# The output's store, the sums for 1/z and the split of the scaled output: three moves in the order of a pooled-attention and SoLU-FFN kernel

## The chip, the core and the metric

The kernel runs on one core of one Trainium2 chip. The metric is the device time of one execution in microseconds (us); lower is better. The engines are named as the profile names them: PE is the matrix engine (TensorE) and PEld its weight loads, DVE is VectorE, ACT is ScalarE, POOL is GpSimd, and SP is the engine whose queue issues nearly all DMAs here; SPq marks its issuing instructions.

## What is computed

```python
kv_flat = kv.reshape(B, H//4, 4, W//4, 4, C).mean(axis=(2, 4)).reshape(B, -1, C) @ w_sr
s = q @ kv_flat.T / sqrt(C)
a = exp(s - s.max(-1)); a /= a.sum(-1) + 1e-9
x = a @ kv_flat
h = x @ w_in
e = exp(h - h.max(-1))
solu = h * e / (e.sum(-1) + 1e-9)
ln = (solu - mean(solu)) / sqrt(var(solu) + 1e-6) * g_ln
out = ln @ w_out
```

There are 4 batches of 12288 queries of 128 features; pooling leaves 768 keys per batch; the hidden width is 1024. All is float32 outside the kernel. Inside, most products are made of a high and a low 16-bit part, so that one product in float32 becomes three in 16 bits.

## The kernel before

The 49152 queries are cut into 384 tiles of 128, and four tiles make a group; there are 96 groups, 24 to a batch. One loop runs over 384 slots. A slot holds the work of one tile in every stage, and each stage is some slots behind the one ahead of it, so that a slot works on some ten different tiles. What follows says which stage works on which tile in the slot `slot`, with `t` for the tile.

- **Scores.** PE multiplies queries by keys into PSUM (`scores_pe`, L386, tile slot + 1). DVE takes the row's maximum `nm` (L402), ACT takes the exponential and its sum `z` (L403) and writes the high half of `phl` (L407), DVE writes the low half (`scores_split`, L415). SP turns `phl` into `pT` by a DMA transpose (`scores_turn`, L422). The four transposes of a group go out in the slots that are 1, 2 and 3 modulo 4, two of them in the last.
- **Values.** PE multiplies `pT` by the values for a whole group at once, in four quarters over four slots (`values`, tile `xa`, L453). The first quarter stands in the slot that is 1 modulo 4 and needs the group's last `pT`, which was issued two slots before. ACT and DVE split the result into `xh` (L459) and `xl` (L464).
- **1/z.** For a group, POOL forms `zz` from `z` (`values_norm`, L479), DVE takes the reciprocal `rz` (`values_recip`, L487), and ACT derives a third column of it (`values_recip_u`, L492). The constant `NORM = 6` puts all three six slots after the slot of the group's last tile, in one that is 1 modulo 4: one slot ahead of the first use of `rz`.
- **Hidden.** PE makes `h` (`hidden_pe`, L505, tile slot - 9). DVE takes the least of the scaled row (`hidden_max`, tile `junkd`, L513, tile slot - 10), ACT the exponential `e` (L529), DVE the product `u` (`hidden_u`, L543, tile slot - 11), ACT the variance (`junk`, L603), and POOL splits `u` into two halves of `uhl` (L560, L566). SP turns `uhl` into `uT` by a DMA transpose (`hidden_turn`, L580).
- **Output.** PE multiplies `uT` by `w_out` into one PSUM bank per group (`final_pe`, tile `o`, L631, tile slot - 13). DVE scales the bank into `ob` in two instructions (`final_half`, L674): tiles 0 and 1 of the group in the slot that is 0 modulo 4, ahead of the product of tile 3, and tiles 2 and 3 in the next slot. Behind the second, SP stores the group's 256 KB (`final_store`, L685).

In the last slot of every group SP also loads the queries of a later group (`q_load`, L345). For batches 1 to 3, keys come in 16 loads of 384 KB each (`kv_load`, L216), begun while the batch before is still worked on; POOL adds them up, and PE, ACT and POOL make keys and values of them in slots listed in `PLAN`.

There is no scheduler: each engine's instructions run in the order in which the loop's body calls the helpers, and SP's DMAs are issued in that order, one queue, first in first out. A DMA whose data isn't ready holds up all those behind it. After slot 383 a hand-written list, `TAIL`, gives the order of what is left.

PSUM: `s` and `h` share three buffers of two banks each, in turn. So PE's `s` of a slot waits for DVE's `u` of the same slot, and PE's `h` of a slot waits for DVE's low half of `phl` of that slot. `xa` and `o` have one bank each. Of `ob` there are two buffers.

Of the kernel before, what the change touches and what calls it, by code (L numbers as in the profile page):

```python
# [21 lines left out]
P = 128  # L22
# [23 lines left out]
XSP = 5  # L46
NORM = 6
LH = 10
LO = 13
# [7 lines left out]
TAIL = """  # L57
U:-1 xa:-1 xh:-1 h:1 o:-4 M:0 xl:-1 J:-1 h:2 hi:-1 E:0 lo:-1 M:1 zz:-1 E:1 o:-3 U:0 h:3
J:0 U:1 zz:0 hi:0 rc:-1 h:4 M:2 ob:-3 rc:0 hi:1 f2:-2 lo:0 rz:-1 E:2 turn:-1 xa:0 turn:0
# [18 lines left out]
def kernel(  # L78
# [63 lines left out]
    state = {}  # L142
# [526 lines left out]
    def final_half(g, half):  # L669
        _, f = state["f", g]  # L670
        if half == 0:
            state["ob", g, 0] = dmt.tile([P, GT, P], F32, tag="ob", name=f"ob_{g}_0")
        js = slice(half * 2, half * 2 + 2)
        nc.vector.scalar_tensor_tensor(  # L674
            state["ob", g, 0][:, js],
            state["po", g][:, half * 256 : half * 256 + 256].rearrange("p (j c) -> p j c", j=2),
            swi,
            f[:, js].unsqueeze(2).to_broadcast([P, 2, P]),
            op0=ALU.mult,
            op1=ALU.mult,  # L680
        )

    def final_store(g, j0=0, j1=GT):
        t0, n = g * GT + j0, j1 - j0
        nc.sync.dma_start(  # L685
            out[t0 * P : (t0 + n) * P, :].rearrange("(j p) c -> p j c", p=P),
            state.pop(("ob", g, j0)),
        )

    def final_out(g):  # L690
        final_half(g, 1)
        final_store(g)

# [182 lines left out]
    def at_last(t, fn, *args):  # L876

        if 0 <= t < NT and t % GT == GT - 1:
            fn(t // GT, *args)

    def at_soon(t, fn):

        at_last(t, fn) if t >= GT else fn(0) if t == GT - 2 else None
# [8 lines left out]
    for slot in range(NT):  # L892
# [20 lines left out]
        at(slot + 1, scores_pe)  # L913
        at_soon(slot - NORM, values_norm)
        at_last(slot - FSC, final_scale)
# [22 lines left out]
        if slot >= LH:  # L938
# [3 lines left out]
            elif slot > LH:  # L942
                for t in (slot - 1, slot):
                    if t > LH and (t % GT == GT - 1) == (t == slot):
                        scores_turn(t)
        at_soon(slot - NORM, values_recip)
        at_soon(slot - NORM, values_recip_u)
        at(i + 1, hidden_pe)
# [5 lines left out]
        at(i - 1, hidden_turn)  # L954
        at_last(slot - LO - 1, final_out)
        at_last(slot - XSP, values_out)
        for st in todo:
# [3 lines left out]
            elif len(st) == 1 and st[0].func not in (*FRONT, *BETWEEN, kv_load):  # L961
                st[0]()
        if slot % GT == GT - 1:
            q_load(slot // GT + 3)
        for st in todo:
# [65 lines left out]
```

## Time and profile before

| | us |
|---|---|
| median of 3 runs | 1854.53 (1848.84 to 1858.07) |
| the profiled execution | 1848.9 |
| its span | 1847.1 |

| engine | busy us | share of the span |
|---|---|---|
| PE | 1821.1 | 99% |
| DVE | 1784.9 | 97% |
| ACT | 1752.8 | 95% |
| POOL | 1613.8 | 87% |

A matmul counts as busy until its modelled end, and the next one starts before that, so PE's share is an upper bound of its work. The granted clock of PE is at full speed in all 40 slices of the span. Issuing a DMA doesn't count as busy: how full SP's queue is has to be read from the timeline of its issues. A row of the timeline gives the start, the duration, the engine, the line, the operation, the tiles written and read, and how many instructions were merged; in brackets the idle time ahead of it and what ended that. A row of the waits gives the total, the number of waits and the longest.

### The profile page before, as it was taken

The numbers are of one execution on the slowest core, as the hardware profiler recorded it, in microseconds if no ns is written. First come the engines' busy times: TensorE is split into PE (matmuls) and PEld (weight loads), VectorE is DVE, ScalarE is ACT, GpSimd is POOL, SyncE is SP. The second block draws the span as 40 slices with busy tenths as digits, with TensorE's granted clock in tenths as the row PEclk, the third lists the DMA queues.
The fourth block names the chain that finished last, engine by engine and source line by source line (L and its number), as shares of the span: only waits on it lengthen the run. The fifth ranks groups of instructions, "written<-read, shape, count | busy, mean of one in ns | idle before, by whom it ended". The sixth has DMA issues, their size and how long they took to land.

```text
span 1847.1 us, 43152 instructions
## 1 busy us (share of the span) xinstructions
PE 1821.1 (99%) x15717; PEld 1179.2 (64%) x15718; DVE 1784.9 (97%) x2729; ACT 1752.8 (95%) x3148; POOL 1613.8 (87%) x1392
## 2 busy tenths in 40 slices
PE   8999999999999999999999999999999999999999
PEld 4566666666666666666666666666666666666666
DVE  7999999999999999999999999999999999999998
ACT  6999999999999999999999999999999999999998
POOL 3899889899998999989988899989888888888887
PEclk9999999999999999999999999999999999999999
DMA  8999999999999999999999999999999999999998
GB/s 300 208 238 233 229 245 234 236 240 245 232 234 240 244 238 241 235 233 238 235 233 234 247 241 241 238 236 231 227 217 230 233 228 223 230 227 231 224 223 179
DMA packets 1473253, 431.80 MB, mean 234 GB/s; under 512 B 1400977, under 2 KB 1454353, under 8 KB 1472785
## 3 DMA queue, kind: packets, MB, share of 16 engines
q1 hardware_dynamic: 1472752, 428.98, 114.1%
q8 instruction: 124, 2.03, 0.5%
q14 instruction: 89, 0.72, 0.1%
q10 hardware_dynamic: 288, 0.07, 0.0%
HBM read 52.50 MB, written 25.17 MB: 42 GB/s over the span
## 4 chain that ended last, share of the span: by engine, by line
PE 63%; DVE 13%; ACT 7%; POOL 7%; issue 7%; DMA 3%; DVEq 0%; POOLq 0%; ACTq 0%
PE o L631 19%; PE h L505 18%; PE xa L453 13%; PE s L386 13%; DVE junkd L513 3%; DVE nm L402 3%; POOL uhl L566 3%; DVE phl L415 2%; ACT e L529 2%; DMA pT<-phl 2%; ACT junk L603 2%; POOL uhl L560 2%; ACT phl L407 2%; DVE u L543 1%; DVE ob L674 1%
## 5 line engine op out<-in xcount | busy, mean ns | idle before, releaser
L566 POOL TENSOR_TENSOR uhl<-u,uhl 128x1024 f16<-128x1024 f32 x382 | 815.1, 2134 | 31.7 <-ACT uhl L558 0.2
L631 PEld LDWEIGHTS <-uT 128*128 128x128 f16 x9072 | 537.1, 98 | 91.9 <-DMA uT<-uhl 7.0
L631 PE MATMUL o<-wch,uT 128*128 128x128 f16 x6048 | 568.0, 219 | 1.3 <-DMA uT<-uhl 1.3
L631 PE MATMUL o<-wcl,uT 128*128 128x128 f16 x3024 | 525.9, 219 | 0.0
L560 POOL TENSOR_SCALAR uhl<-u 128x1024 f16<-128x1024 f32 x377 | 393.5, 1044 | 136.2 <-DVE u L543 131.1
L543 DVE SCALAR_TENSOR_TENSOR u<-h,rz,e 128x1024 f32<-128x1024 f32 x384 | 491.2, 1279 | 16.0 <-ACT e L529 3.6
L513 DVE TENSOR_SCALAR_CACHE_REDUCE junkd<-h,rz 128x1024 bf16<-128x1024 f32 x384 | 491.5, 1280 | 1.4 <-PE h L505 1.0
L529 ACT ACTIVATE e<-h,nm,rz 128x1024 f32<-128x1024 f32 x384 | 459.0, 1195 | 1.0 <-DVE junkd L513 1.0
L603 ACT ACTIVATE junk<-u,su 128x1024 bf16<-128x1024 f32 x384 | 437.8, 1140 | 0.2 <-DVE u L543 0.2
L402 DVE TENSOR_REDUCE nm<-s 128x1 f32<-128x768 f32 x384 | 365.7, 952 | 23.3 <-PE s L386 20.8
L453 PE MATMUL xa<-pT,vh 128*128 128x512 f16 x1152 | 373.5, 379 | 6.6 <-DMA pT<-phl 4.0
L403 ACT ACTIVATE s<-s,nm 128x768 f32<-128x768 f32 x384 | 335.9, 875 | 41.9 <-DVE nm L402 37.1
L415 DVE SCALAR_TENSOR_TENSOR phl<-s,phl 128x768 f16<-128x768 f32 x384 | 366.3, 954 | 4.5 <-ACT phl L407 4.3
L407 ACT ACTIVATE phl<-s 128x768 f16<-128x768 f32 x384 | 311.0, 810 | 11.7
L505 PEld LDWEIGHTS <-xh 128*128 128x128 f16 x1536 | 144.8, 97 | 191.7 <-issue 26.7
L386 PE MATMUL s<-kh,qh 128*128 128x384 f32 x768 | 248.0, 404 | 0.1
L505 PE MATMUL h<-w_in_h,xh 128*128 128x512 f16 x768 | 228.2, 379 | 3.5 <-DVE rz L487 2.4
L505 PE MATMUL h<-w_in_h,xl 128*128 128x512 f16 x768 | 228.4, 379 | 0.0
L505 PE MATMUL h<-w_in_l,xh 128*128 128x512 f16 x768 | 228.3, 379 | 0.0
L453 PE MATMUL xa<-pT,vl 128*128 128x512 f16 x576 | 218.3, 379 | 0.0
L386 PE MATMUL s<-kc,ql 128*128 128x384 bf16 x768 | 187.8, 326 | 7.4 <-DVE phl L415 4.4
L386 PE MATMUL s<-kl,qf 128*128 128x384 bf16 x768 | 192.2, 332 | 0.1
(127 smaller groups left out, 1707.2 us busy)
## 6 DMA issues: line engine op xcount, KB each, us to landing
kv<-in_kv_dram SPq DMA_DIRECT2D x64, 384.0 KB, 4.3
qf<-in_q_dram SPq DMA_DIRECT2D x96, 256.0 KB, 3.3
out_dram<-ob SPq DMA_DIRECT2D x95, 256.0 KB, 2.8
pT<-phl SPq DMA_TRANSPOSE x384, 3.8
uT<-uhl SPq DMA_TRANSPOSE x378, 4.4
raw_in<-in_moe_w_in_dram SPq DMA_DIRECT2D x1, 1024.0 KB, 5.4
raw_out<-in_moe_w_out_dram SPq DMA_DIRECT2D x1, 1024.0 KB, 8.6
out_dram<-ob SPq DMA_DIRECT2D x1, 192.0 KB, 2.0
```

The costliest lines, as they stand in the source:

```text
L386: nc.tensor.matmul(s[:, half, :384], lh[:, ts], rh[:, half * 384 : (half + 1) * 384], start=n == (t == 0), stop=n == 2,)
L402: nc.vector.tensor_reduce(nm, s, axis=AX.XY, op=ALU.max, negate=True)
L415: nc.vector.scalar_tensor_tensor(phl[:, 1], state.pop(("s", t)), SC, phl[:, 0], op0=ALU.mult, op1=ALU.subtract)
L453: nc.tensor.matmul(xa, v[:, c, :], pT[:, :, a * NKC + c, :], start=n == 0, stop=n == len(seq) - 1)
L505: nc.tensor.matmul(h[:, hs], lh[:, ts], rh[:, hs], start=n == 0, stop=n == 2)
L513: nc.vector.tensor_scalar(junk, state["h", t], state["rz", g][1][:, j : j + 1], None, op0=ALU.mult, op1=ALU.min, accum_out=nm,)
L529: nc.scalar.activation(e, state["h", t], AF.Exp, bias=nm, scale=state["rz", g][0][:, js], accum_out=state["z2", g][:, js],)
L543: nc.vector.scalar_tensor_tensor(u, state.pop(("h", t)), state["rz", g][2][:, j : j + 1], state.pop(("e", t)), op0=ALU.mult, op1=ALU.mult, ...
L560: nc.gpsimd.tensor_scalar(uhl[:, 0, :], u, 1.0, 1.0, op0=ALU.mult, op1=ALU.mult)
L566: nc.gpsimd.tensor_tensor(uhl[:, 1, :], u, uhl[:, 0, :], op=ALU.subtract)
L603: nc.scalar.activation(junk, u, AF.Square, scale=-float(DFF), bias=su, accum_out=state["v3", g][:, j : j + 1],)
L631: nc.tensor.matmul(po[:, ts], uT[:, a * NFC + c, :], w[:, c, :], start=start, stop=stop)
```

## The change

Three things move, and no instruction is added or taken away:

- The store of a group goes out two slots later, in the slot that is 3 modulo 4, behind that slot's transposes and ahead of the load of queries.
- `zz` is formed three slots sooner, in the slots 2 modulo 4, and `rz` (DVE) and its third column (ACT) one slot sooner, in the slots 0 modulo 4. In DVE's order the reciprocal now stands ahead of the first piece of the scaled output instead of ahead of the second.
- The output is scaled in pieces of three tiles and one instead of two and two.

```diff
-NORM = 6
+ZSUM = 3
+ZREC = 5
...
-        js = slice(half * 2, half * 2 + 2)
+        j0, n = ((0, 3), (3, 1))[half]
+        js = slice(j0, j0 + n)
         nc.vector.scalar_tensor_tensor(
             state["ob", g, 0][:, js],
-            state["po", g][:, half * 256 : half * 256 + 256].rearrange("p (j c) -> p j c", j=2),
+            state["po", g][:, j0 * P : (j0 + n) * P].rearrange("p (j c) -> p j c", j=n),
             swi,
-            f[:, js].unsqueeze(2).to_broadcast([P, 2, P]),
+            f[:, js].unsqueeze(2).to_broadcast([P, n, P]),
...
-    def final_out(g):
-        final_half(g, 1)
-        final_store(g)
...
-        at_soon(slot - NORM, values_norm)
+        at_soon(slot - ZSUM, values_norm)
...
-        at_soon(slot - NORM, values_recip)
-        at_soon(slot - NORM, values_recip_u)
+        at_soon(slot - ZREC, values_recip)
+        at_soon(slot - ZREC, values_recip_u)
...
-        at_last(slot - LO - 1, final_out)
+        at_last(slot - LO - 1, final_half, 1)
...
         if slot % GT == GT - 1:
+            at_last(slot - LO - 3, final_store)
             q_load(slot // GT + 3)
```

In `TAIL` the step `zz:-1` is gone, because the loop now reaches it. All rows of the orders below are of the first batch; a number behind a tile's name is its tile or group, and the one behind that can be passed over.

SP's queue before, from one load of queries to the next (the store is that of group 13, the `pT` that of group 17):

```order
L345 DMA qf_19_4726<-in_q_dram 128x512
L580 DMA_TRANSPOSE uT_57_4793<-uhl_57_4745 128x16x128
L216 DMA kv_2_1_4798<-in_kv_dram 128x768
L422 DMA_TRANSPOSE pT_17_4758<-phl_68_4732 128x12x128
L580 DMA_TRANSPOSE uT_58_4875<-uhl_58_4820 128x16x128
L685 DMA out_0_dram<-ob_13_0_4767 128x4x128
L422 DMA_TRANSPOSE pT_17_4758<-phl_69_4803 128x12x128
L580 DMA_TRANSPOSE uT_59_4946<-uhl_59_4898 128x16x128
L422 DMA_TRANSPOSE pT_17_4758<-phl_70_4885 128x12x128
L422 DMA_TRANSPOSE pT_17_4758<-phl_71_4951 128x12x128
L580 DMA_TRANSPOSE uT_60_5017<-uhl_60_4967 128x16x128
L345 DMA qf_20_5019<-in_q_dram 128x512
```

The same stretch of SP's queue in the change:

```order
L346 DMA qf_19_4730<-in_q_dram 128x512
L581 DMA_TRANSPOSE uT_57_4801<-uhl_57_4749 128x16x128
L217 DMA kv_2_1_4806<-in_kv_dram 128x768
L423 DMA_TRANSPOSE pT_17_4762<-phl_68_4736 128x12x128
L581 DMA_TRANSPOSE uT_58_4875<-uhl_58_4824 128x16x128
L423 DMA_TRANSPOSE pT_17_4762<-phl_69_4811 128x12x128
L581 DMA_TRANSPOSE uT_59_4949<-uhl_59_4901 128x16x128
L423 DMA_TRANSPOSE pT_17_4762<-phl_70_4884 128x12x128
L423 DMA_TRANSPOSE pT_17_4762<-phl_71_4954 128x12x128
L581 DMA_TRANSPOSE uT_60_5020<-uhl_60_4970 128x16x128
L687 DMA out_0_dram<-ob_13_0_4775 128x4x128
L346 DMA qf_20_5023<-in_q_dram 128x512
```

The store has passed five transposes: three of `pT`, among them the group's last (`phl_71`), and two of `uT` (59 and 60). What stands behind the load of queries has the same work ahead of it as before.

DVE before, in the slots 100 and 101, from the first piece of the scaled output to the second and the maximum behind it:

```order
L674 SCALAR_TENSOR_TENSOR ob_21_0_7135<-o_21_6924,swi_100,f2_21_7040 128x256
L402 TENSOR_REDUCE nm_101_7168<-s_101_7106 128x1
L543 SCALAR_TENSOR_TENSOR u_90_7173,su_90_7174<-h_90_7061,rz_22_6893,e_90_7121 128x1024
L464 SCALAR_TENSOR_TENSOR xl_23_7165<-xa_23_6906,xh_23_7163 128x512
L513 TENSOR_SCALAR junkd_91_7194,nm2_91_7193<-h_91_7128,rz_22_6893 128x1024
L415 SCALAR_TENSOR_TENSOR phl_101_7171<-s_101_7106,phl_101_7171 128x768
L487 RECIPROCAL rz_23_7185<-zz_23_7184 128x8
L674 SCALAR_TENSOR_TENSOR ob_21_0_7135<-o_21_6924,swi_100,f2_21_7040 128x256
L402 TENSOR_REDUCE nm_102_7248<-s_102_7177 128x1
```

The same stretch of DVE in the change:

```order
L488 RECIPROCAL rz_23_6973<-zz_23_6972 128x8
L676 SCALAR_TENSOR_TENSOR ob_21_0_7143<-o_21_6924,swi_100,f2_21_7043 128x384
L403 TENSOR_REDUCE nm_101_7176<-s_101_7110 128x1
L544 SCALAR_TENSOR_TENSOR u_90_7181,su_90_7182<-h_90_7064,rz_22_6680,e_90_7125 128x1024
L465 SCALAR_TENSOR_TENSOR xl_23_7173<-xa_23_6910,xh_23_7171 128x512
L514 TENSOR_SCALAR junkd_91_7198,nm2_91_7197<-h_91_7136,rz_22_6680 128x1024
L416 SCALAR_TENSOR_TENSOR phl_101_7179<-s_101_7110,phl_101_7179 128x768
L676 SCALAR_TENSOR_TENSOR ob_21_0_7143<-o_21_6924,swi_100,f2_21_7043 128x128
L403 TENSOR_REDUCE nm_102_7247<-s_102_7185 128x1
```

The reciprocal and 128 elements of the scaled output have gone from between `phl_101` and `nm_102` to the place ahead of `nm_101`.

## Rows read from the trace of the kernel before

**Rows 1.** Page, part 1: busy time, share of the span and instructions of each engine.
```profile
PE 1821.1 (99%) x15717; PEld 1179.2 (64%) x15718; DVE 1784.9 (97%) x2729; ACT 1752.8 (95%) x3148; POOL 1613.8 (87%) x1392
```

**Rows 2.** Windows: busy us by engine, granted clock, DMA share, GB/s; key loads until 1240.
```profile
117.00:1240.00 1123.00, 1113.09 (x9687) 721.63 (x9686) 1094.93 (x1675) 1074.39 (x1929) 1020.05 (x879) 1.00 1.19 238
1240.00:1786.00 546.00, 545.41 (x4776) 355.92 (x4774) 536.73 (x823) 528.35 (x949) 465.26 (x394) 1.00 1.13 227
```

**Rows 3.** Waits of PE from 117 to 1240 us: total us, times, longest us.
```profile
PE xa L453 <- DMA pT<-phl: 4.0, 8, 1.0
PE xa L453 <- DVE ob L674: 2.2, 2, 1.1
PE o L631 <- DMA uT<-uhl: 1.3, 4, 0.5
PE h L505 <- DVE rz L487: 1.1, 4, 0.4
```

**Rows 4.** Waits of PE from 1240 to 1786 us, the only row.
```profile
PE h L505 <- DVE rz L487: 0.6, 2, 0.4
```

**Rows 5.** Timeline of SP's issues from a store on, and the store four groups later.
```profile
946.63 0.53 SPq L685 DMA_DIRECT2D out_dram<-ob  x1
947.26 1.47 SPq L422 DMA_TRANSPOSE pT<-phl  x1
...
956.81 0.53 SPq L345 DMA_DIRECT2D qf<-in_q_dram  x1
957.45 2.68 SPq L580 DMA_TRANSPOSE uT<-uhl  x1
...
1021.92 0.53 SPq L685 DMA_DIRECT2D out_dram<-ob  x1
```

**Rows 6.** Page, part 6: DMA issues, KB each, median us to landing.
```profile
kv<-in_kv_dram SPq DMA_DIRECT2D x64, 384.0 KB, 4.3
out_dram<-ob SPq DMA_DIRECT2D x95, 256.0 KB, 2.8
```

**Rows 7.** Timeline of DVE in one group without loads of keys, and the next group's first.
```profile
1453.98 0.96 DVE L402 TENSOR_REDUCE nm<-s 128x1 f32<-128x768 f32 x1
1455.07 1.28 DVE L543 SCALAR_TENSOR_TENSOR u<-h,rz,e 128x1024 f32<-128x1024 f32 x1
...
1458.35 0.47 DVE L674 SCALAR_TENSOR_TENSOR ob<-o,swi,f 128x256 f32<-128x256 f32 x1
1458.74 0.94 DVE L402 TENSOR_REDUCE nm<-s 128x1 f32<-128x768 f32 x1
...
1462.61 0.95 DVE L415 SCALAR_TENSOR_TENSOR phl<-s,phl 128x768 f16<-128x768 f32 x1
1463.48 0.19 DVE L487 RECIPROCAL rz<-zz 128x8 f32<-128x8 f32 x1
1463.59 0.43 DVE L674 SCALAR_TENSOR_TENSOR ob<-o,swi,f 128x256 f32<-128x256 f32 x1
1463.94 0.95 DVE L402 TENSOR_REDUCE nm<-s 128x1 f32<-128x768 f32 x1
...
1472.50 0.96 DVE L402 TENSOR_REDUCE nm<-s 128x1 f32<-128x768 f32 x1
```

**Rows 8.** Timeline of PE in the same group: scores, values and hidden products.
```profile
1458.16 0.50 PE L386 MATMUL s<-kl,qf 128*128 128x384 bf16 x2
...
1463.45 0.38 PE L453 MATMUL xa<-pT,vh 128*128 128x512 f16 x1
1463.71 0.59 PE L505 MATMUL h<-w_in_h,xh 128*128 128x512 f16 x2
```

**Rows 9.** Timeline of ACT in the same group: the end of an exponential, and `xh`.
```profile
1454.77 0.19 ACT L529 ACTIVATION_READ_ACCUMULATOR e<-h,nm,rz 128x1 f32 x1
...
1459.35 0.60 ACT L459 ACTIVATE xh<-xa 128x512 f16<-128x512 f32 x1 [0.17 <-PE xa L453]
```

**Rows 10.** Timeline of POOL in the same group: the split of `u`.
```profile
1466.18 1.04 POOL L560 TENSOR_SCALAR uhl<-u 128x1024 f16<-128x1024 f32 x1 [1.94 <-DVE u L543]
```

More of the change, by code (lines that the diff above doesn't have):

```diff
@@ L57 @@
 TAIL = """
-U:-1 xa:-1 xh:-1 h:1 o:-4 M:0 xl:-1 J:-1 h:2 hi:-1 E:0 lo:-1 M:1 zz:-1 E:1 o:-3 U:0 h:3
+U:-1 xa:-1 xh:-1 h:1 o:-4 M:0 xl:-1 J:-1 h:2 hi:-1 E:0 lo:-1 M:1 E:1 o:-3 U:0 h:3
 J:0 U:1 zz:0 hi:0 rc:-1 h:4 M:2 ob:-3 rc:0 hi:1 f2:-2 lo:0 rz:-1 E:2 turn:-1 xa:0 turn:0
```

## The prediction

> **What bounds the kernel now.** The page's busy times come first: PE has 99% of the span, DVE 97%, ACT 95% [rows 1]. No engine has room, so the time can only come out of PE's waits, and the next view is PE's waits by stretch. I cut the span where the loads of keys end, near 1240 us. Ahead of it PE waits 4.0 + 2.2 + 1.3 + 1.1 = 8.6 us in 18 waits [rows 3]; behind it, to 1786 us, 0.6 us in 2 [rows 4]. These rows understate: a matmul is drawn for 0.38 us while the next starts 0.21 later (two together last 0.59 [rows 8]), so a wait shows up to 0.17 us short. With 18 × 0.17 = 3.1 the first stretch holds at most 11.7 us of waits. Of the 18, 10 are of `xa`, and the largest row names its cause: the transposed scores `pT` had not landed. The second `xa` row names DVE's `ob`, which `xa` doesn't read; I count it as the same lateness.
>
> Why `pT` is late is read from two more views. The timeline of SP's issues shows stores at 946.63 and, four groups later, at 1021.92 [rows 5]: 18.82 us per group. Between them the issues stand end to end, with about 0.1 us between one and the next (947.26 follows 946.63 + 0.53); there is no gap in which the queue waits for data. The timeline of DVE in a group without loads of keys gives the pace that the engines can hold: from 1453.98 to 1472.50, 18.52 us [rows 7]. So from 117 to 1240 us the DMA queue is the slowest, by 0.30 us per group, and PE's waits are this difference showing whenever PE has used up its lead. A sum of bytes agrees. A group issues four transposes of 384 KB and four of 512 KB (128 × 12 × 128 and 128 × 16 × 128 halves of 2 bytes), a store and a load of queries of 256 KB each, and two loads of keys of 384 KB [rows 6] in every three groups: 4352 KB, or 4.46 MB. At the 238 GB/s that moved there [rows 2] that is 18.7 us. Without keys it is 4.19 MB, at 227 GB/s 18.5 us: the queue then merely keeps up with PE.
>
> **The change part by part.** *The store.* It keeps its 256 KB and its issue; five transposes pass it. In a queue that is never empty they go out sooner by what the store holds it up, at least its issue (947.26 - 946.63 = 0.63 us [rows 5]), at most its share by bytes (262 KB at 238 GB/s = 1.1 us). I take 1.1, since the queue is short of transfer and not of issues. But the queue's total per group is the same, and what stands behind the load of queries (two `uT`, the keys, the first `pT`) is as late as before. A queue of 18.82 us per group still lets PE do one group in 18.82. What is gained is lead: the `xa` that PE catches up with last may come 1.1 us sooner, once, and that lead stays to the end, because behind 1240 us PE hardly waits. So -1.1 us, not -1.1 per group. The lower end is 0, if one of the two `uT` that gain nothing is what PE catches up with last (4 of its waits are on `uT` already); the upper end is all 11.7 us, if the order and not the bytes made the queue slow. SP is also moved past one wait: `ob` is long done when the store now comes up, so the store can't hold the queue. `ob` is held two slots longer; its buffer is wanted again only two groups on, and the store lands in 2.8 us [rows 6].
>
> *The reciprocal and the third tile on DVE.* The reciprocal takes 0.11 us of DVE's order (1463.48 to 1463.59), a piece of two tiles 0.35 (1463.59 to 1463.94), and `phl` with 768 elements 0.87 (1462.61 to 1463.48) [rows 7]: 0.52 more for 512 more elements, about 0.13 for a tile. So 0.11 + 0.13 = 0.24 us go from behind `phl` in the slots 1 modulo 4 to ahead of `nm` in the same slots. DVE's sum is unchanged. Now `nm` starts at 1458.74, 0.39 behind the first piece; in the change at 1458.35 + 0.11 + 0.35 + 0.13 = 1458.94, 0.20 later. From there to the end of `phl` at 1463.56 DVE has no gap, and PE's `h` at 1463.71 waits for that end: the `xa` ahead of it began at 1463.45 and would have let `h` start at 1463.66 [rows 8]. So in the first such group PE's `h` is 0.20 us later. Does that come back in every group? The chain that leads to `phl` is not PE's any more. It runs from `u` at 1455.07, which waits for the exponential that ends at 1454.96 on ACT [rows 9]; `nm` ahead of it began at 1453.98 and, at the 0.87 us of `phl` with as many elements, would have let `u` start at 1454.85. ACT in turn follows from DVE's `nm` at 1463.94 of the group before. The second piece is shorter by the same 0.24 us, so that `nm` comes at 1458.94 + 4.74 (1463.48 - 1458.74) + 0.35 - 0.13 = 1463.90 instead of 1463.94. DVE and ACT thus return to where they were, with PE up to 0.20 us later and waiting less next time. I take 0.2 us once, lost in rounding, and keep 0.20 per group as the other end.
>
> *The rest.* ACT's third column goes ahead of `xh`, into 0.17 us in which ACT waits for PE [rows 9]; without that cover it would cost some tenths on `xh`, which `xl` awaits more than a microsecond later. `zz` goes ahead of the split of `u` in the slots 2 modulo 4, where POOL idles 1.94 us [rows 10]; if POOL is behind there, it delays the queries' low part by as much as it did one slot sooner. Both 0, as is the step taken out of the tail's list, whose work is done just ahead of it. PE's next group of `o` waits for the second piece, which ends sooner by the 0.24 less the 0.20.
>
> The sum is 1848.9 - 1.1 = 1847.8 us against the profiled execution, which lies 5.6 us under the median of the runs shown, 1854.5. I forecast the median: 1854.5 - 1.1 = **1853.4 us**. A difference of half a per cent, 9.3 us, is about what a measurement of this kernel can tell from none.
>
> The Trainium skill, DMA: Bandwidth & Descriptors, in its section Latency and other measured facts, gives 261 GB/s for DMA transposes with a strided middle dimension. By that the 4.46 MB of a group would take 17.1 us, an estimate from that page, the queue would have 1.4 us to spare, its lateness would be one of order, and the sum would be -11.7 us. The trace differs: the queue moves 238 GB/s while its issues stand end to end, and I go by that.
>
> **The rivals.** *Order is what makes the queue late, and the waits vanish.* The store writes to HBM between transposes that stay on the chip; beside the load of queries it may overlap with it, and the queue need save only 0.30 of 18.82 us per group to stop being the bound. For it: a transpose behind a copy is long (2.68 us behind the load of queries, 1.47 behind the store [rows 5]), so copies are not simply additive. Against it: bytes alone explain the pace in both stretches [rows 2]. It gives 1854.5 - 11.7 = 1842.8 us at most, 1847 if only the ten waits of `xa` go (6.2 + 10 × 0.17 = 7.9). The page of the Trainium skill named above would make this the likeliest case.
>
> *DVE becomes late in every group.* If `u` in the slots 0 modulo 4 is not held by ACT but by `nm`, PE's lateness returns on DVE and the 0.20 us are paid in each group. The point is the wait at 1455.07: `u` could start at 1454.85 and has 0.22 us of cover, hardly more than the 0.20 us that are added. In the 60 groups with loads of keys the queue's 0.30 us would hide it; in the other 34 or so it costs 34 × 0.20 = 6.8 us: 1861.3 us. If it adds to the queue instead of hiding behind it, it is 94 × 0.20 = 18.8 us: 1873.3 us. For it: `h` stands right behind `phl` already. Against it: DVE's and ACT's own round comes out unchanged.
>
> **How the numbers follow.** No change but the 1.1 us of lead: 0.69. The queue loses its excess: 0.20, of which 0.17 counts as faster, since the median run shown, 5.6 us above the profiled one, has more than 11.7 us to win, and 0.03 as same. DVE late: 0.11, of which 0.02 stays within half a per cent (the 34 groups alone) and 0.09 lies beyond. So faster 0.17, same 0.69 + 0.03 + 0.02 = 0.74, slower 0.09. The runs shown spread by -5.7 and +3.5 us about their median. The range goes from 1844, most of the first rival, to 1862, the lower end of the second; the forecast's own range is 1849 to 1858.
>
> **What would show it.** In the profile of the change, stores in SP's timeline should still be 18.8 us apart between 117 and 1240 us, end to end, with the five transposes sooner against PE; DMA in that stretch at 238 GB/s; PE's waits there still near 8 us in sum, with `uT` taking over from `pT`. The first rival would show gaps in SP's issues ahead of 1240 us and groups of 18.5 us. The second would show groups of 18.7 us behind 1240, where now they take 18.52, and PE's `h` waiting for `phl` by 0.2 us more in each. I am wrong on the mechanism if SP's pace changes by over 0.15 us per group, or if the stretch behind 1240 us grows or shrinks by over 3 us.

## The result, and the profile after

The changed kernel takes 1862.77 us in the median (1858.12 to 1866.52) where the kernel before takes 1854.53: a ratio of 1.0056, 95% interval [1.0044, 1.0067]. It is slower: by the ratio about 10 us, while the two medians lie 8.2 us apart. The forecast was 1853.4 with no difference that can be measured. The profiled execution has a span of 1861.2 us.

The first part of the page of the changed kernel, busy time, share and instructions of each engine, as [rows 1]:

```profile
PE 1830.4 (98%) x15717; PEld 1178.6 (63%) x15718; DVE 1782.6 (96%) x2729; ACT 1758.9 (95%) x3148; POOL 1614.1 (87%) x1392
```

The instructions are the same and so is their work, so the time went into waits. Where, the starts of PE's scores tell. The rows of PE's timeline that begin group 7 (the first key loads are under way), group 67 (they have ended) and group 95 (the last), in the kernel before:

```profile
135.01 0.33 PE L386 MATMUL s<-kc,ql 128*128 128x384 bf16 x1
...
1265.66 0.33 PE L386 MATMUL s<-kc,ql 128*128 128x384 bf16 x1
...
1786.12 0.33 PE L386 MATMUL s<-kc,ql 128*128 128x384 bf16 x1
```

and in the changed kernel:

```profile
135.97 0.33 PE L387 MATMUL s<-kc,ql 128*128 128x384 bf16 x1
...
1277.33 0.33 PE L387 MATMUL s<-kc,ql 128*128 128x384 bf16 x1
...
1800.06 0.33 PE L387 MATMUL s<-kc,ql 128*128 128x384 bf16 x1
```

From group 7 to 67 it takes 1141.36 us instead of 1130.65, and from 67 to 95 522.73 instead of 520.46. So 10.7 us were lost while keys are loaded and 2.3 behind. These are one execution of each kernel, 14.1 us apart in span; by the ratio of all runs the loss is about 10.4 us, so that some 8 lie ahead of group 67. The two stretches are read for every kernel that follows.

The windows of the changed kernel, as [rows 2]: full clock (1.00) and 236 GB/s instead of 238 while keys are loaded, 226 instead of 227 behind.

```profile
117.00:1250.00 1133.00, 1116.45 (x9676) 719.80 (x9676) 1092.78 (x1676) 1077.58 (x1928) 1020.36 (x878) 1.00 1.19 236
1250.00:1800.00 550.00, 549.20 (x4786) 356.77 (x4785) 537.82 (x824) 531.86 (x953) 466.68 (x397) 1.00 1.13 226
```

PE's waits from 117 to 1250 us, as [rows 3]:

```profile
PE o L632 <- DMA uT<-uhl: 8.8, 13, 1.3
PE xa L454 <- DMA pT<-phl: 2.9, 5, 1.2
PE h L506 <- DVE phl L416: 2.0, 7, 0.5
PE xa L454 <- DVE phl L416: 1.4, 2, 0.7
```

`pT` got better (4.0 to 2.9 us), `uT` took its place and much more (1.3 to 8.8): the transposes of `uT` behind the load of queries are late now (all 13 waits are for `uT` of the tiles 1 and 2 of a group, the two that stand next behind it). SP's issues of the changed kernel, from a store on, and the store four groups later, as [rows 5]:

```profile
1003.05 0.58 SPq L687 DMA_DIRECT2D out_dram<-ob  x1
1003.72 0.50 SPq L346 DMA_DIRECT2D qf<-in_q_dram  x1
1004.33 3.10 SPq L581 DMA_TRANSPOSE uT<-uhl  x1
...
1079.49 0.57 SPq L687 DMA_DIRECT2D out_dram<-ob  x1
```

The issues still stand end to end, but four groups now take 76.44 us, 19.11 each, where it was 18.82 [rows 5]. Taken over the 60 groups, from the first `pT` of group 7 to that of group 67, SP's pace went from 18.82 to 18.99 us. The `uT` behind the pair took 3.10 us here and 2.68 in [rows 5]; over the groups 10 to 63 it takes 3.02 us from its issue to the next one instead of 2.65.

DVE in one group behind the key loads, as [rows 7] (the brackets give the idle time ahead and what ended it):

```profile
1466.54 0.96 DVE L403 TENSOR_REDUCE nm<-s 128x1 f32<-128x768 f32 x1 [0.16 <-PE s L387]
1467.43 1.28 DVE L544 SCALAR_TENSOR_TENSOR u<-h,rz,e 128x1024 f32<-128x1024 f32 x1
...
1470.78 0.19 DVE L488 RECIPROCAL rz<-zz 128x8 f32<-128x8 f32 x1
1470.89 0.57 DVE L676 SCALAR_TENSOR_TENSOR ob<-o,swi,f 128x384 f32<-128x384 f32 x1
1471.37 0.95 DVE L403 TENSOR_REDUCE nm<-s 128x1 f32<-128x768 f32 x1
...
1476.11 0.34 DVE L676 SCALAR_TENSOR_TENSOR ob<-o,swi,f 128x128 f32<-128x128 f32 x1
1476.37 0.95 DVE L403 TENSOR_REDUCE nm<-s 128x1 f32<-128x768 f32 x1
...
1485.13 0.96 DVE L403 TENSOR_REDUCE nm<-s 128x1 f32<-128x768 f32 x1 [0.16 <-PE s L387]
```

The group takes 1485.13 - 1466.54 = 18.59 us instead of 18.52. The first `nm` of the group now waits for PE's scores, and `u` follows it at once (0.89 us later), where in [rows 7] it came 1.09 later and had waited for ACT's exponential. Over the groups 70 to 93 DVE idles for the scores ahead of the first `nm`, by over 0.15 us, in all 24; in the kernel before in 3. PE loses its time at one matmul of a group only, the `h` behind `phl`:

```profile
1476.01 0.38 PE L454 MATMUL xa<-pT,vh 128*128 128x512 f16 x1
1476.34 0.59 PE L506 MATMUL h<-w_in_h,xh 128*128 128x512 f16 x2
```

It starts 0.33 us behind the `xa` ahead of it, where [rows 8] have 0.26. In those groups (the 22 of them with the same matmuls) no other matmul of PE's order shifts by over 0.012 us on average; this one shifts by 0.065.

### The profile page after: what moved, and what is told of

Its sections match the earlier page's. It is cut to its first block, busy times and chain, and to the rows that moved or that the text cites. A ratio compares the mean times of both kernels' runs of the same rounds, so it can differ in the third digit from the quotient of the medians.

```text
span 1861.2 us, 43073 instructions
## 1 busy us (share of the span) xinstructions
PE 1830.4 (98%) x15717; PEld 1178.6 (63%) x15718; DVE 1782.6 (96%) x2729; ACT 1758.9 (95%) x3148; POOL 1614.1 (87%) x1392
## 4 chain that ended last, share of the span: by engine, by line
PE 78%; DMA 7%; POOL 6%; DVE 6%; issue 2%; ACT 1%; POOLq 0%; DVEq 0%; ACTq 0%
PE o L632 23%; PE h L506 22%; PE xa L454 16%; PE s L387 16%; DMA uT<-uhl 6%; POOL uhl L567 3%; DVE phl L416 2%; DMA pT<-phl 2%; POOL uhl L561 1%; DVE nm L403 1%; DVE junkd L514 1%; POOL ka L228 1%; DVE u L544 1%; DVE ob L676 0%; POOL ql L363 0%
```

## The experiments

Every kernel below ran on the chip beside the kernel before (its median there 1848.6 to 1850.9 us). All that is read from the traces stands in one table: the two stretches in us, by the rows of PE's scores shown above, and SP's pace in us per group from group 7 to 67. Pace is the mean over these 60 groups; over so many SP and PE keep step, so it goes with the first stretch and does not tell by itself which of the two is slow. Stretches and pace come from one profiled execution of each kernel, time and ratio from 4 to 12. Executions of the kernel before spread from 1845 to 1855 us. The second stretch is steady (520.4 to 520.7 us in 15 kernels), so that spread lies in the first, where a few us mean something only if the ratio bears them out.

| kernel | time, us | ratio to before [95%] | 7 to 67 | 67 to 95 | pace |
|---|---|---|---|---|---|
| before | | | 1130.7 | 520.5 | 18.82 |
| the change | 1862.77 | 1.0056 [1.0044, 1.0067] | 1141.4 | 522.7 | 18.99 |
| store_only | 1853.95 | 1.0026 [1.0014, 1.0039] | 1135.7 | 520.4 | 18.89 |
| store_back | 1854.96 | 1.0029 [1.0018, 1.0039] | 1136.7 | 522.5 | 18.91 |
| recip_only | 1850.84 | 1.0013 [1.0003, 1.0022] | 1132.5 | 520.5 | 18.83 |
| pieces_only | 1849.61 | 1.0004 [0.9991, 1.0016] | 1130.3 | 520.7 | 18.80 |
| recip_3 | 1850.69 | 1.0008 [0.9996, 1.0020] | 1131.4 | 520.7 | 18.81 |
| dve_pad | 1865.61 | 1.0087 [1.0074, 1.0100] | 1139.4 | 528.2 | 18.95 |
| nokeys_before | 1837.70 | 0.9937 [0.9919, 0.9956] | 1119.6 | 520.5 | 18.65 |
| nokeys_store | 1838.08 | 0.9938 [0.9921, 0.9955] | 1119.5 | 520.4 | 18.65 |
| nokeys_after | 1845.50 | 0.9981 [0.9972, 0.9991] | 1125.1 | 522.5 | 18.75 |
| store_mid | 1851.60 | 1.0010 [0.9996, 1.0023] | 1130.1 | 520.5 | 18.80 |
| store_zero | 1847.91 | 0.9994 [0.9983, 1.0004] | 1126.8 | 520.6 | 18.73 |
| q_store | 1868.83 | 1.0100 [1.0076, 1.0123] | 1151.6 | 520.5 | 19.20 |
| q_beside | 1862.21 | 1.0066 [1.0045, 1.0087] | 1139.8 | 520.4 | 18.93 |
| keys_q | 1851.67 | 1.0011 [1.0000, 1.0022] | 1133.2 | 520.6 | 18.83 |
| keys_st | 1861.02 | 1.0061 [1.0049, 1.0073] | 1138.6 | 520.6 | 18.92 |
| keys_apart | 1858.34 | 1.0056 [1.0034, 1.0078] | 1140.8 | 520.4 | 18.96 |
| after_keys_apart | 1865.03 | 1.0082 [1.0063, 1.0101] | 1142.8 | 522.5 | 19.02 |
| mended | 1847.56 | 0.9995 [0.9986, 1.0005] | 1128.1 | 520.6 | 18.76 |

### Which part of the change

At first there were two theories: Q, that the store beside the load of queries slows SP's queue while keys are loaded, and D, that DVE's moves are the loss. *store_only* is the kernel before with the store moved as in the change:

```diff
-        at_last(slot - LO - 1, final_out)
+        at_last(slot - LO - 1, final_half, 1)
...
         if slot % GT == GT - 1:
+            at_last(slot - LO - 3, final_store)
             q_load(slot // GT + 3)
```

> The kernel before with the store alone moved to where the change puts it. Theory Q (the store beside the load of queries slows SP's queue while keys are loaded; DVE's moves cost little): most of the loss is here, 1860 to 1862 us beside 1854.5; the stretch with loads of keys takes 18.95 to 19.0 us per group instead of 18.82, and a group without loads of keys stays at 18.52. Theory D (DVE's moves make every group late and the queue follows): 1853 to 1855 us, 18.82 and 18.52 us per group, as before.

The times in these expectations were set beside 1854.5 us; here the kernel before took 1849.7, so the ratio decides. It loses 0.26%, all of it ahead of group 67, where PE's waits have the change's pattern (4 and 1.3 us in [rows 3]):

```profile
PE o L631 <- DMA uT<-uhl: 8.2, 11, 1.4
PE xa L453 <- DMA pT<-phl: 2.0, 5, 0.9
```

*store_back* is the change with the store put back behind the second piece:

```diff
         at_last(slot - LO - 1, final_half, 1)
+        at_last(slot - LO - 1, final_store)
...
-            at_last(slot - LO - 3, final_store)
```

> The change with the store alone put back behind the second piece of the output; the sums, the reciprocal and the pieces of three and one stay. Theory Q: 1855 to 1857.5 us; the stretch with loads of keys at 18.8 us per group, a group without them at 18.60 as in the change. Theory D: 1861 to 1863 us, and the stretch with loads of keys at 19.0.

It loses 0.29%. So Q and D each name a half: 0.26 + 0.29 = 0.55, and the change loses 0.56. *recip_only* takes the kernel before with `NORM` replaced by `ZSUM = 3` and `ZREC = 5` alone, *pieces_only* takes it with the pieces of three tiles and one alone.

> The kernel before with the sums and the reciprocal alone sooner. 0.11 us goes ahead of the scores' maximum in the slots 1 modulo 4. Theory Q: a group without loads of keys takes 18.52 to 18.56 us, the whole within 2 us of the kernel before. Theory D: about half of the loss, 1857 to 1859 us.

> The kernel before with the pieces of three tiles and one alone. 0.13 us goes ahead of the scores' maximum in the slots 1 modulo 4. Theory Q: a group without loads of keys takes 18.52 to 18.56 us, the whole within 2 us of the kernel before. Theory D: about half of the loss, 1857 to 1859 us.

Alone, neither costs anything behind group 67 (520.5 and 520.7 us); together they cost 2.0. The sooner sums and reciprocal alone lose 0.13%, with an interval that begins at 0.03%. Behind the loads the price is not in either move but in their sum.

### DVE: 0.24 us ahead of one maximum

*recip_3* keeps both moves of store_back but puts the reciprocal yet a slot sooner, so that only 0.13 us of the 0.24 stands ahead of the `nm` in question:

```diff
-ZREC = 5
+ZREC = 4
```

(on store_back; the two steps of the tail that the loop now reaches, `rc:-1` and `rz:-1`, go.)

> Edit: the change with the store put back, and the reciprocal and its third column one slot sooner still, in the slots 3 modulo 4, so that only the third tile's 0.13 us is added ahead of the maximum in the slots 1 modulo 4, and the reciprocal's 0.11 us lies ahead of the maximum of a slot 0 modulo 4. Theory C (each of the two is within DVE's cover ahead of that one maximum, their sum of 0.24 is not): a group takes 18.52 to 18.54 us behind group 67, the stretch from group 67 on 520.5 to 521, and the time is within 2 us of the kernel before. Rival (DVE has no cover there in a slot 0 modulo 4 either, or 0.24 us sooner costs wherever it is put): 18.58 to 18.60 us per group, 522.5 us, and 5 us above the kernel before, as store_back.

520.7 us behind group 67, and 1850.69 us in all, a ratio whose interval holds 1: DVE's loss is gone. Its timeline in one group behind the key loads:

```profile
1468.90 0.94 DVE L403 TENSOR_REDUCE nm<-s 128x1 f32<-128x768 f32 x1
1469.98 1.28 DVE L544 SCALAR_TENSOR_TENSOR u<-h,rz,e 128x1024 f32<-128x1024 f32 x1
...
1473.27 0.19 DVE L488 RECIPROCAL rz<-zz 128x8 f32<-128x8 f32 x1
...
1477.75 0.61 DVE L676 SCALAR_TENSOR_TENSOR ob<-o,swi,f 128x384 f32<-128x384 f32 x1
1478.28 0.95 DVE L403 TENSOR_REDUCE nm<-s 128x1 f32<-128x768 f32 x1
...
1487.41 0.95 DVE L403 TENSOR_REDUCE nm<-s 128x1 f32<-128x768 f32 x1
```

1487.41 - 1468.90 = 18.51 us: the same instructions as in store_back, with the reciprocal (and ACT's third column) one slot sooner.

*dve_pad* asks whether the queue hides such a lateness while keys are loaded. It is the kernel before with two more reciprocals, whose result nothing uses, in front of the first piece:

```diff
             state["ob", g, 0] = dmt.tile([P, GT, P], F32, tag="ob", name=f"ob_{g}_0")
+            pad = tiny.tile([P, GT], F32, tag="padr", name=f"padr_{g}", bufs=1)
+            for _ in range(2):
+                nc.vector.reciprocal(pad, f)
```

> Edit: the kernel before, with two more reciprocals of 128x4 (about 0.1 us each, their result unused) ahead of the first piece of the scaled output, so 0.2 us more of DVE ahead of the maximum in the slots 1 modulo 4, and nothing taken away behind. Theory H (my prediction's second rival: the queue hides a lateness of the engines while keys are loaded): the stretch from group 67 on grows by X = 2 to 6 us (0.07 to 0.20 us for each of 28 groups), the stretch from group 7 to 67 by less than half of X times 60/28, since the engines' own pace there (18.66 without loads, nokeys_before) plus X/28 only just reaches the queue's 18.82. Theory A (queue and engines add up, as in store_back): the stretch from 7 to 67 grows by X times 60/28, within a fifth, and the time by about 3.1 X.

The two reciprocals take more than the 0.2 us that were meant, here 1488.82 - 1488.53 = 0.29:

```profile
1488.53 0.38 DVE L675 RECIPROCAL padr<-f 128x4 f32<-128x4 f32 x2
1488.82 0.45 DVE L677 SCALAR_TENSOR_TENSOR ob<-o,swi,f 128x256 f32<-128x256 f32 x1
```

The stretch from 67 on grew by 7.7 us, 0.275 for each group: nearly all of what was added is paid. Of the 0.24 us in store_back a third is paid; there the same time was taken away again behind `phl`, here nothing is. Had the stretch from 7 to 67 paid the same per group, it would have grown by 7.7 × 60 / 28 = 16.5; it grew by 8.7. Neither theory's number fits (H said under 8.3, A about 16.5), and H is much the nearer: about half is hidden. The slower of engines and queue alone would have given 1119.6 (nokeys_before, below) + 16.5 = 1136.1 us, and the stretch took 1139.4. What shows of it in PE's waits from 117 to 1250 us, against 1.1 and 4.0 us in [rows 3], is that the waits for DVE rise and those for `pT` fall:

```profile
PE h L505 <- DVE rz L487: 7.5, 33, 0.6
PE xa L453 <- DMA pT<-phl: 2.9, 5, 1.0
```

For store_back the same sum goes: 5.4 us by its ratio, of which 2.0 lie behind group 67, leave 3.4 ahead of it, where 2.0 × 60 / 28 = 4.3 would be all (without the loads of keys the same moves cost 5.5 there, below); the interval of the ratio (3.3 to 7.2 us in all) doesn't tell half from all there. The 6.0 us of the table are one execution, 2.7 us above the median of its kernel.

### The queue: is it short of room?

The three kernels without keys leave out 15 of 16 loads of each of the batches 1 to 3; the sums take the first load's keys in their place. *nokeys_before* is the kernel before, *nokeys_after* the change, *nokeys_store* is store_only, each with:

```diff
     def kv_load(b, pos):
+        if pos:
+            state["kv", b, pos] = state["kv", b, 0]
+            return
```

> The kernel before with one load of keys in sixteen for batches 1 to 3; the other fifteen are left out, and the sums take the first load's keys in their place. The queue then has room throughout: 1831 to 1838 us, the groups at 18.52 us but for those in which keys are made, PE's waits for pT and uT under 2 us.

> The change with the same loads of keys left out. With the queue out of the way only DVE's moves are left. Theory Q (each group without DMA waits takes 18.60 instead of 18.52 us, and the store costs only while keys are loaded): 6 to 8 us over the same kernel before without keys (92 groups of 0.07 to 0.08 us). If the store costs without keys too: 9 us or more. If DVE's moves were the loss of the queue's stretch alone: under 3 us.

> Edit: the kernel before with the store moved as in the change and nothing else, and the same 15 of 16 loads of keys per batch left out as in nokeys_before (the sums reuse the first load). Theory N with a queue that keeps up: the transpose behind the load of queries is still 0.3 us longer, but without keys the queue has room for it: time within 1.5 us of nokeys_before (1837.7), the queue's pace within 0.05 us of 18.65. Rival (the store's loss does not depend on the load of the queue): 3 us or more above nokeys_before, as with keys.

Without the loads of keys the kernel before takes 18.65 us per group there; the engines' own work on keys is still in it. The loads thus cost 1130.7 - 1119.6 = 11.1 us, and 0.63% or 11.6 us by the ratio, near the prediction's upper bound of PE's waits (11.7). In nokeys_before the queue moves less:

```profile
117.00:1240.00 1123.00, 1120.67 (x9776) 729.82 (x9776) 1102.27 (x1691) 1085.01 (x1949) 1028.71 (x888) 1.00 1.13 228
```

The moved store costs nothing that shows with this room (0.9938 beside 0.9937), so its price is a price of the queue. nokeys_after loses 5.5 us from group 7 to 67 and 2.0 behind, which is then all of it DVE's moves.

That the queue is what is short can also be read from when a `uT` is issued, counted from the end of POOL's second half of its `uhl`. For the tiles 40 to 267 that is 3.14 us in the mean in the kernel before and 0.46 in nokeys_before; it is 2.90 in store_zero, 3.50 in store_only, 3.70 in the change and 4.12 in q_store (store_zero and q_store follow below). So the data wait for the queue. Behind the loads of keys, tiles 272 to 359 of the kernel before, it is 0.35: there the queue waits for the data.

### Which places in the queue are dear

Theory N said that plain copies side by side make the transposes behind them long; theory P, at first, that any store moved behind transposes costs. *store_mid* moves the store by one slot only, behind the `uT` of the slots 2 modulo 4 (`at_last(slot - LO - 2, final_store)`). *q_beside* leaves the store and moves the load of queries directly behind it:

```diff
         at_last(slot - LO - 1, final_out)
+        if slot % GT == 1 and slot > GT:
+            q_load(slot // GT + 2)
...
-        if slot % GT == GT - 1:
-            q_load(slot // GT + 3)
```

> The kernel before with the store alone moved one slot later, behind the transpose of u in the slots 2 modulo 4: it passes one pT and one uT, and no other copy stands beside it. Theory N (copies side by side cost: the store next to the load of queries makes the transpose behind them and those of u late): within 2 us of the kernel before, pT waits of PE a little less, uT waits no more than 4 us. Theory P (any store that is moved behind transposes costs, because the transposes of u that gain nothing are those PE waits for): about half of the 4.2 us that the store alone cost.

> The kernel before with the store where it was and the load of queries moved directly behind it, two slots later. Theory N: the two copies side by side cost as much here as in the change, 3 to 6 us over the kernel before, with pT behind them late. Theory P: nothing is moved behind transposes but the queries, which have slots to spare; within 2 us of the kernel before.

store_mid costs nothing, against that P; q_beside costs 0.66%, which spoke for N. If N held, the loads of keys should also gain by being apart. In `kv_plan`, *keys_apart* has `ADDS[pos] - 6` for `ADDS[pos] - 8`, and *after_keys_apart* is the change with the same edit.

> Edit: the kernel before, with every load of keys two slots later, in the slots 2 modulo 4, so that two transposes of uT and one of pT stand between it and the load of queries, and one of pT and one of uT between it and the store. No two plain copies are close to each other any more; bytes and issues are the same. Theory N (plain copies close to each other make the transposes behind them long): the queue's pace from group 7 to 67 falls from 18.82 to 18.70 us per group or less, PE's waits for pT from 9 to under 6 us, the time is 2 to 6 us below the kernel before (ratio 0.997 to 0.999). Rival B (bytes alone set the pace of the queue in groups with keys): pace and time as before, within 1 us. The stretch from group 67 on is 520.5 us in both.

> Edit: the change, with every load of keys two slots later as in keys_apart; the store still stands directly beside the load of queries. Theory N: the load of keys no longer follows the pair of store and queries with one transpose between, part of the queue's loss returns: the queue's pace falls from 18.99 to about 18.88 us per group and the time lies 3 to 7 us below the changed kernel (1862 down to 1855 to 1859, beside 1850 of the kernel before). Theory D (what is left is DVE's chain) agrees that 5 us remain. Rival B: 1862, within 1 us, the pace unchanged.

Both came out 6 us and more above what N said: keys_apart is 0.56% slower than the kernel before, after_keys_apart 0.82%, where the change has 0.56%. No two copies are close to each other there, so N as a rule falls. SP's issues in keys_apart show where it went: the two `pT` behind the load of keys, of which the second is the group's last and the one that `xa` needs, take 4.17 us together; in the next group, without a load of keys, such a pair took 3.13 (from its start to the next issue 4.59 and 3.31 in the mean of the groups 13 to 65, and 3.55 with a load in the kernel before). Below, PE's waits from 117 to 1250 us: those for `pT` rose from 4.0 to 10.7.

```profile
1012.95 0.57 SPq L216 DMA_DIRECT2D kv<-in_kv_dram  x1
1013.61 4.17 SPq L422 DMA_TRANSPOSE pT<-phl  x2
...
1031.90 3.13 SPq L422 DMA_TRANSPOSE pT<-phl  x2
```

```profile
PE xa L453 <- DMA pT<-phl: 10.7, 9, 1.7
```

Three kernels then put the same copies at the other places: *keys_q* the loads of keys directly behind the load of queries (`ADDS[pos] - 9`, its bounds 7 and -33), *keys_st* directly behind the store (`ADDS[pos] - 7`, 9 and -31), *store_zero* the store behind the first `uT` that follows the load of queries:

```diff
-        at_last(slot - LO - 1, final_out)
+        at_last(slot - LO - 1, final_half, 1)
+        at_last(slot - LO - 4, final_store)
```

(and `st:-4` at the head of the tail.) Theory O: a load close behind another load is cheap. (Its 1.50 us for a load in the kernel before are no firm price: a group with a load takes 1.86 us more than one without if groups are cut at the load of queries, and 0.87 if they are cut at the store.) Theory L: a load's distance to the group's last `pT` counts. P now means that a store costs where a `uT` stands right behind it and the load of queries.

> Edit: the kernel before, with every load of keys one slot sooner, so that it stands directly behind the load of queries in the slots 3 modulo 4 instead of behind the transpose of uT after it. Theory N (plain copies side by side make the queue slow): the queue's pace from group 7 to 67 rises from 18.82 to 18.90 to 19.0 us per group, the time is 5 to 10 us above the kernel before. Theory O (a load close behind another load from HBM is cheaper, which is why a load of keys cost 1.50 us of the queue in the kernel before and 1.8 to 1.9 where it stood alone in keys_apart and in q_beside): pace 18.70 to 18.80, the time 1 to 6 us below the kernel before. Theory L (what counts is how far a load stands ahead of the group's last pT, not its neighbours): within 1.5 us of the kernel before.

> Edit: the kernel before, with every load of keys one slot later, directly behind the store in the slots 1 modulo 4; four transposes (pT, uT, pT, pT) are behind it until the group's last pT has gone out. Theory N: slower by 5 to 10 us, pace 18.90 to 19.0, for the pair side by side. Theory O: the load stands alone among loads, a store is no load, so it costs 1.8 us instead of 1.5: pace about 18.95, as keys_apart, 7 to 10 us slower, and the transposes right behind the pair carry it. Theory L: the load is ahead of the group's last pT by one transpose more than in keys_apart: pace 18.85 to 18.92, 2 to 6 us slower, and PE waits for pT more than before (over 12 us in sum).

> Edit: the kernel before, with the store three slots later, in the slots 0 modulo 4, behind that slot's uT, so that it stands between the load of queries (one uT ahead of it) and the load of keys, which in two groups of three follows it directly. Theory N: side by side with a load in two groups of three: pace 18.86 to 18.92, 2 to 6 us slower than the kernel before. Theory O (loads that follow each other share something, a store between them breaks it up): the load of keys costs 1.8 us instead of 1.5, pace about 18.95, 6 to 9 us slower. Theory P (a store costs where a uT is directly behind it and the load of queries, as in the change): pT stands behind it here, so within 1.5 us of the kernel before.

keys_q is 0.11% slower with an interval that begins at no difference (medians 0.8 us apart): nearest to L, and against N and O. keys_st is 0.61% slower, which N and O had, and L not; its PE waits for `uT` (6.4 us in 8 waits, 7 of them for the `uT` next behind the load of keys) more than for `pT` (3.7). store_zero has the store directly ahead of a load of keys in two groups of three, and shows no difference (0.9994, interval 0.9983 to 1.0004), against N and O; P stands. Its PE's waits from 117 to 1250 us:

```profile
PE o L631 <- DMA uT<-uhl: 3.0, 6, 1.2
PE xa L453 <- DMA pT<-phl: 1.5, 4, 0.9
```

The last of this row, *q_store*, is store_only with the pair turned round: `final_store` stands behind `q_load`, not ahead of it.

> Edit: the kernel before with the store moved alone, but directly behind the load of queries instead of directly ahead of it; the same five transposes pass it as in the change. Theory P (the price is paid by a uT directly behind a pair of copies, in whichever order): pace from group 7 to 67 18.87 to 18.92 us, time 3 to 6 us above the kernel before, the issue of the uT behind the pair about 3.0 us instead of 2.65. Rival S (the price is that of a load of queries that stands behind a store): the load goes out as before, pace 18.72 to 18.82, time within 1.5 us of the kernel before.

It loses 1.00%, four times as much as the same pair the other way. S, by which the price is that of a load of queries behind a store, falls; P has the direction, and not the size. SP's issues at the pair, and below them PE's largest group of waits from 117 to 1250 us:

```profile
1028.13 0.53 SPq L345 DMA_DIRECT2D qf<-in_q_dram  x1
1028.72 0.45 SPq L685 DMA_DIRECT2D out_dram<-ob  x1
1029.27 2.91 SPq L580 DMA_TRANSPOSE uT<-uhl  x1
```

```profile
PE o L631 <- DMA uT<-uhl: 15.7, 20, 2.2
```

What is shown: with the same bytes and the same number of issues the order of SP's queue alone makes the kernel up to 1.00% slower, SP's pace 18.73 to 19.20 us per group in the executions profiled, and in each of the three kernels in which the store stands directly beside the load of queries (store_only, q_beside, q_store) it is slower. In all five kernels that are slower by the order of the queue alone, the waits that grew are for transposes that stand behind the copies in question: the two `uT` behind the load of queries in store_only (all 11 waits) and q_store (16 of 20), the `uT` behind the load of keys in keys_st, `pT` in q_beside (9.4 us) and keys_apart. What is not shown is a rule for all places: no theory here fits keys_apart, keys_st, store_zero and q_store together, and why the queue slows stays open.

### Both losses mended

*mended* is the change with `ZREC = 4` as in recip_3 and the store at `slot - LO - 4` as in store_zero; sums, pieces and the rest stay.

> Edit: the change with both of its losses mended as the runs so far suggest: the reciprocal one slot sooner still (slots 3 modulo 4, as recip_3), and the store one slot later (slots 0 modulo 4, behind that slot's uT, as store_zero); the sums for 1/z and the pieces of three tiles and one stay as in the change. If the two losses are the whole difference and are independent: stretch from group 67 on 520.5 to 521 us, pace from 7 to 67 18.70 to 18.82 us, time 1847 to 1852 us, 9 to 13 us below the change and within 2 us of the kernel before. Rival (they interact): the pace stays above 18.88 or a group behind 67 takes 18.56 us or more.

Both losses are gone, and within the interval they were the whole difference: pace 18.76 us, 520.6 us behind group 67. PE's waits for DMA in it, from 117 to 1250 us:

```profile
PE o L632 <- DMA uT<-uhl: 2.9, 5, 0.9
...
PE xa L454 <- DMA pT<-phl: 0.8, 1, 0.8
```

Against the kernel before, mended (0.9995) and store_zero (0.9994) are 1 us faster in the estimate and within the interval of no difference; no kernel with all loads of keys beats it measurably.

## Why the prediction was wrong

The forecast failed in two steps, and by the prediction's own test: SP's pace changed by 0.18 us per group, over the 0.15 that it named. That test was blunt: of the 0.18 the store alone makes 0.08 (store_only), which would have passed, and DVE's lateness slows SP's pace too (dve_pad). The stretch behind the loads grew by 2.3 us, within the 3 allowed, and still held a loss in every group: 522.73 / 28 = 18.67 us per group instead of 18.59.

- **"The queue's total per group is the same" (the store).** This is the step that failed first. The store did leave `pT` its lead, and `uT` did take over, as foreseen. But the total rose from 18.82 to 18.99 us, of which the store alone made 18.89. The mistake was to take end-to-end issues and a sum of bytes for a rate that no order can change: the bytes fitted the pace of one order only. I gave this term 0 to -11.7 us; its true value is +4.8 (0.26%), on the side that I had excluded. That what stands behind the load of queries "is as late as before" is refuted by the row of `uT` (3.10 against 2.68; 3.02 against 2.65 in the mean). What makes the queue slower in this order stays open.
- **The 0.30 us by which the queue is the slowest** were too many. The 18.52 us of [rows 7] are one group without work on keys; where keys are made, the engines alone need 18.65 (nokeys_before). The queue was short by 18.82 - 18.65 = 0.17 us per group, so a lateness of the engines had 0.13 us less room to hide in than I counted.
- **The first rival** had the right mechanism, that the order sets the queue's pace beside the bytes, and the wrong sign for this order. Of its waits only those of `pT` shrank. In store_zero they shrank to 1.5 us, and the kernel was no faster by a difference that shows (0.9994). By the 261 GB/s of the Trainium skill, DMA: Bandwidth & Descriptors, Latency and other measured facts, the queue would have, as an estimate, 1.4 us to spare. The trace does not agree: where `uT` waited for the queue, it moved 238 GB/s in the kernel before and 236 in the change, and the room was not there.
- **"0.2 us once, lost in rounding" (DVE).** The 0.20 us were right (1471.37 - 1470.78 is 0.59 us where [rows 7] have 0.39). DVE did return as foreseen: the third `nm` of a group comes 1476.37 - 1466.54 = 9.83 us behind the first, not later than the 9.96 of [rows 7], and dve_pad, where nothing is taken away to return, pays nearly all that it adds. Wrong was the other half of that sentence, PE "waiting less next time": behind the loads PE has only 0.6 us of waits in 546 [rows 4] and could not give the lateness back. I looked for the cover at `u`, 0.22 us against 0.20, and overlooked that PE's lateness comes back through the scores: the first `nm` of the next group waits for `s`, starts later and takes the cover from `u`, which now follows after 0.89 us instead of 1.09. So 0.07 to 0.08 us come back in every group, a third of the 0.20 that I kept as the other end. Alone, each move costs nothing there (520.5 and 520.7 us); in recip_3, with 0.13 us ahead of that `nm`, the loss is gone.
- **The second rival** was this mechanism, with too high a price (0.20 per group) and the right warning (cover "hardly more than the 0.20"). Its clause that the queue hides it in the groups with key loads is half right: dve_pad shows about half hidden there. Why not all is not shown; a likely reason is that the queue is short in a part of those groups only, since in the kernel before SP takes 19.45 us for a group with a load of keys and 17.58 for one without (means of the groups 13 to 65).
- **The rest, 0:** the sums and the third column cost no more than recip_only as a whole, 0.13% (up to 0.22 by its interval), the pieces nothing that shows, the tail nothing (61.0 and 61.2 us from the last group's scores to the end). The 11.7 us of PE's waits were near what the loads cost (11.1).

The range reached 1862 and the median is 1862.77; the chance of slower, 0.09, was far too low, because the store's term had no upper end above zero.

## What to carry to other kernels

A DMA queue whose issues stand end to end is not a constant of so many bytes: price a moved copy from both sides, and look for what stands right behind it at its new place. On engines that take turns in a ring, a move of a few tenths has to be followed once round the ring, through every engine, to the place where it started; the cover that counts is the smallest one on the way. Two moves that cost nothing alone may cost something together, so test them together and apart.

## What the runs showed of the hardware that was not expected

- The same store and load of queries side by side cost 0.26% with the store first and 1.00% with the load first; with one `uT` between them and the load first (store_zero), nothing.
- By order alone, with equal bytes, the queue takes 18.73 to 19.20 us for a group in the executions profiled, and the kernel is up to 1.00% slower. With a load of keys ahead of them two `pT` take 4.17 us in one group, and 3.13 in the next, which has no load.
- DVE, 96% busy, takes 0.11 or 0.13 us ahead of one maximum without a loss that shows behind the loads of keys, and 0.24 with a loss of 0.07 to 0.08 us in each group, if the same time goes from behind it. Where 0.29 were added and nothing was taken away (dve_pad), 0.275 were lost.
